# Linear attention and a SiLU MLP on one core: chunk 0 in two token parts, one more column group by Strassen's scheme, last sums per half

## The chip, the cores and the metric

The kernel runs on one core of one Trainium2 chip. The metric is the device time of an execution in microseconds (us). Eleven executions of the kernel before took 271.12 to 277.2 us, with a median of 275.72.

Engines are named as in the profile: PE (TensorE, matrix products), PEld (its weight loads), DVE (VectorE), ACT (ScalarE), POOL (GpSimd), SP (SyncE, which here only issues DMAs).

## The reference

Eight batches of 8 heads, 576 tokens, head size 64; then a two-layer MLP over all 4,608 tokens.

```python
q_s = softmax(q, over the head's 64 elements)
k_s = softmax(k, over the 576 tokens)
kv  = einsum('bhsd,bhse->bhde', k_s, v)          # 64 x 64 per head
x   = einsum('bhsd,bhde->bhse', q_s, kv)         # heads side by side: (4608, 512)
h   = x @ w_in                                   # (4608, 2048)
g   = h * (1.0 / (1.0 + exp(-h)))                # silu
out = g @ w_out                                  # (4608, 512), float32
```

## The kernel before

**Attention, per batch.** q, k and v of a batch are loaded as 128-partition tiles `qt`, `kt`, `vt` (one buffer each, so that a load waits for the last reader of the batch before). ACT takes the exponential (`exp`, L106) in two halves of four heads each (`cc` = 0, 1), DVE sums q's rows (`qsum`, L120 and L121), and `qnorm` (L126) multiplies; POOL does that for batches 1 to 7. `tr_dma` (L137) has a DMA transpose the normed q into `qT`; batch 0 is transposed on PE instead (`tr`, L149). `vcast` puts v as bf16 beside a column of ones, `kv` (L168) multiplies exp(k) with it, `kvcopy` (L180, L181) divides by the sums. `xt` (L203) multiplies qT by kv and `xtcopy` (L221, L223) writes the result to `XT`, x transposed, which is the MLP's input.

**The MLP, per chunk.** The tokens are cut into 9 chunks. XT of chunk 0 is made per batch, with 576 tokens, and worked in two pieces of 320 and 256 columns; chunk 1 brings 448 more, and the rest 512 each. (The second layer always takes 512 tokens.) The hidden 2,048 columns are 16 blocks `fb` of 128; four groups `g` of them, each two blocks of the lower and the two matching ones of the upper half, are the unit of Strassen's scheme.

- Chunks 0 and 1 run every block plainly: `mm1` (L233: four matmuls, 512 wide or the piece's width) and `act1`, in which ACT takes a tanh and DVE completes the silu (L247, L259).
- From chunk 2 on, some groups are plain (`std`: two in chunk 2, one in chunks 3 to 8; there ACT takes the silu at L263) and the others go by Strassen's scheme in Winograd's form: seven products of half size instead of eight. `product1` (L316) makes product k with four matmuls of 256 columns. Its left sides are blocks of `W1` or of the sums `TX` of such blocks (`vsum`, L291); its right sides are quarters of XT or their sums `XS` (`xsum`, L273 to L279: S1 = A10 + A11, S2 = S1 - A00, S3 = A00 - A10, S4 = A01 - S2). `sum1` (L333, L339, L341) adds the products up on DVE, one copy per group on DVE or ACT, and `silu1` (L355) writes `GT`.
- The second layer of chunk 0 is plain (`mm2`, L476). For chunks 1 to 8 it is Strassen's scheme too: `presum` (L369 to L375) makes the sums `SW` and rewrites a quarter of GT in place, `wsum` (L387) makes the sums `TW` of `W2` once, `product` (L411) multiplies in two halves `a` of 128 tokens, `after` (L428 and others) adds up on DVE, and `qstore` (L462, L465) has SP issue two DMAs per result, one for each half of the partitions.

The sums of a presum or xsum can run on DVE or POOL. MP and WP tiles are in the 8 PSUM banks: six in the ring that first-layer products, kv and xt share, two for the second layer.

**The order** is written out by hand in `PLAN`: for each chunk, steps with positions (`put`), sorted by position into a list, and issued to the engines in that order. Every engine works its instructions strictly in order. Positions of the second layer of chunk t (`y`, `ya`, `pb`) are in the list of chunk t + 1; the attention of batch b is in list b - 1. `order` is the sequence of (group, product); `xs`/`xe`, `pa`/`pae` and `pb`/`pbe` are positions and engines (0 DVE, 1 POOL) of xsum and of the presums of the first and the second half; `ex`, `qs`, `qn`, `tp`, `ox`, `oc` are positions of exp, qsum, qnorm, transpose, xt and xtcopy; `lq`, `lk`, `lv` of loads.

**The start.** SP issues q, k, v of batch 0 in halves (L97): q0, q1, k0, v0, k1, v1. POOL waits for v0 by a copy of one element (`gate`, L527) and then issues the weights (L516, L522) and batch 1, each casting weights to bf16:

```python
load_w1(0); load_w1(1); load_w2(0); load_w1(2); load_w2(1); load(1, "qt", q, eng=nc.gpsimd)
load_w1(3); load(1, "kt", k, eng=nc.gpsimd); load_w2(2); load(1, "vt", v, eng=nc.gpsimd); load_w2(3)
```

PE runs 24 warm-up matmuls (`heat`, L544), and eight more between the first steps.

Of the kernel before, what the change touches and what calls it, by code (L numbers as in the profile page):

```python
# [15 lines left out]
PLAN = {  # L16
    0: {'y': [5.5, 6.5, 7.5, 8.5, 8.5, 9.5, 10.5, 11.5, 13.5, 13.8, 14.5, 15.5, 15.6, 15.7, 15.9, 22.5], 'ex': [8.9, 10.9, 12.9, 13.4], 'qs': [9.92, 11.4], 'qn': [10.43, 11.41], 'vs': [14.45, 15.05], 'ks': [15.65, 15.75], 'kc': [15.651, 15.751], 'lq': 14.06, 'tp': 12.9, 'ox': [16.35, 16.6], 'oc': [16.36, 18.61], 've': [2, 2]},
    1: {'ex': [0.9, 4.4, 5.9, 5.4], 'qs': [3.9, 4.9], 'qn': [4.91, 5.91], 'vs': [9.3, 10.9], 'ks': [12.4, 13.9], 'kc': [13.41, 14.91], 'lq': 10.45, 'lk': 12.4, 'lv': 15.41, 'tp': 11.4, 'ox': [16.4, 23.6], 'oc': [17.91, 23.61], 've': [1, 1], 'pa': [13.1, 17.7, 18.3], 'pae': [1, 0, 0]},
    2: {'std': 2, 'order': [(3, 1), (2, 1), (2, 6), (3, 6), (2, 2), (2, 7), (3, 2), (3, 7), (3, 5), (2, 5), (2, 4), (3, 3), (3, 4), (2, 3)], 'y': [-2.5, 1.5, 3.5, 4.5, 5.5, 7.5, 9.5, 11.5, 14.0, 15.5, 17.5, 19.0, 20.0, 21.0], 'ex': [-2.6, 0.41, 2.92, 0.43], 'qs': [2.9, 3.9], 'qn': [5.91, 5.91], 'vs': [3.42, 12.4], 'ks': [8.9, 16.4], 'kc': [10.91, 16.41], 'lq': -0.55, 'lk': -2.1, 'lv': 14.41, 'tp': 7.4, 'ox': [18.4, 19.4], 'oc': [18.91, 19.41], 'sl': [0.5, 1.5, 3, 3, 4.5, 8.5, 7, 7], 'add': {(3, 2): 17.02, (2, 7): 13.55, (3, 1): 10.02, (3, 6): 11.55, (2, 5): 17.55, (2, 3): 21.55, (3, 3): 19.55}, 'act': {(2, 6): 13.02, (2, 4): 19.02, (2, 3): 25.02, (2, 5): 17.55, (3, 2): 14.55, (3, 3): 23.02, (2, 1): 11.55, (3, 1): 9.55, (2, 7): 16.02}, 's1': {2: 0, 3: 0}, 'xs': [0.4, 0.9, 7.9, 4.4], 'pa': [16.45, 23.95, 19.45], 'ya': {3: 22.45, 6: 5.5, 5: 15.95, 2: 7.95}, 'm1': [1, 0], 'pb': [-0.4, 0.2, 2.1, 2.2, 2.8], 'xe': [0, 1, 1, 1], 'pae': [1, 1, 1], 'pbe': [0, 0, 0, 0, 0], 've': [1, 2]},
}  # L20
STEADY = {'std': 1, 'order': [(1, 1), (1, 6), (1, 2), (1, 7), (1, 5), (2, 1), (2, 6), (1, 4), (1, 3), (2, 2), (2, 7), (2, 5), (3, 1), (2, 4), (3, 6), (2, 3), (3, 7), (3, 2), (3, 5), (3, 4), (3, 3)], 'y': [1.5, 3.5, 5.5, 7.5, 9.5, 10.0, 15.5, 16.5, 17.5, 18.0, 22.0, 23.5, 24.2, 24.6], 'ex': [-5.1, -0.59, -4.08, -4.57], 'qs': [5.4, 6.4], 'qn': [5.91, 6.41], 'vs': [0.4, 7.42], 'ks': [11.9, 17.4], 'kc': [15.91, 17.41], 'lq': 9.95, 'lk': 16.9, 'lv': 9.41, 'tp': 8.9, 'ox': [22.4, 22.4], 'oc': [22.91, 23.41], 'sl': [2.0, 2.0, 6.5, 4.0], 'add': {(2, 2): 17.02, (1, 2): 6.55, (3, 2): 20.55, (3, 1): 16.55, (3, 7): 21.02, (1, 5): 9.55, (3, 5): 22.55}, 'act': {(1, 5): 12.02, (2, 6): 12.02, (1, 2): 7.02, (3, 1): 19.02, (1, 6): 9.02, (1, 1): 8.02, (3, 3): 25.55, (3, 5): 25.02, (1, 3): 14.02, (2, 2): 15.02, (2, 5): 16.55, (1, 4): 13.02, (3, 7): 23.02, (3, 6): 20.02}, 's1': {1: 1, 2: 0, 3: 0}, 'xs': [-1.6, 0.9, -1.6, 1.4], 'pa': [21.45, 21.95, 23.45], 'pb': [-0.05, 2.46, 2.95, -0.04, 2.95], 'ya': {4: 23.95, 5: 19.45}, 'm1': [0, 0], 'xe': [0, 0, 0, 0], 'pae': [1, 0, 0], 'pbe': [0, 0, 0, 0, 1], 've': [1, 1]}
# [8 lines left out]
def kernel(  # L30
# [71 lines left out]
    def exp(b, src, dst, cc):  # L102
        if dst not in st[b]:
            st[b][dst] = ap.tile([128, J, NG * D], BF16, name=dst, bufs=1)
        o = st[b][dst][:, :, cc * 128:(cc + 1) * 128].rearrange("p j (g d) -> p j g d", d=D)
        nc.scalar.activation(out=o, in_=jgd(st[b][src], cc), func=ACT.Exp)  # L106

    def vcast(b, cc, eng):
        o = vaug.rearrange("p j (g e) -> p j g e", e=E1)[:, :, 2 * cc:2 * cc + 2, 0:D]
        if eng is nc.scalar:  # L110
            eng.copy(out=o, in_=jgd(st[b]["vt"], cc))
        else:
            eng.tensor_copy(o, jgd(st[b]["vt"], cc))

    def qsum(b, cc):
        if "zq" not in st[b]:
            st[b]["zq"] = ap.tile([128, 2, J, 2], FP32, name="zq")
            st[b]["rzq"] = ap.tile([128, 2, J, 2], FP32, name="rzq")
# [69 lines left out]
    def xt(t, cc, tags=("ring", "ring"), dve=0):  # L188
        if t not in XT:
            XT[t] = mp.tile([128, NC, S], BF16, name="XT")  # L190
        for i, (off, size) in enumerate(part[t]):
# [18 lines left out]
            if t == 0:  # L210
                xtcopy(t, cc, dve)
# [292 lines left out]
    for cc in range(2):  # L504
        load(0, "qt", q, cc)
# [182 lines left out]
```

The softmax here doesn't subtract the row's maximum and nothing guards it: scores larger than these inputs give would overflow.

## Time and profile before

| | |
|---|---|
| median of 11 runs | 275.72 us (271.12 to 277.2) |
| the profiled execution | 274.68 us; span of its instructions 272.9 us |
| granted TensorE clock, mean | 0.989 |
| first matmul of chunk 0 | 16.27 us |
| first xt of chunk 2 that uses batch 2 | 69.0 us |
| steady chunk (150.56 to 177.11) | 26.55 us |
| last matmul ends | 268.1 us |
| bytes moved by DMA | 46.48 MB, mean 170 GB/s |

Times count from the span's start. In a group's row stand line, engine, operation, output <- input with partitions x elements and type, the number of instructions, their busy time in us and mean duration in ns; then the idle time of the engine just before them and what ended it. A row of the chain of waits has start, length and what ran. A row of the stages has the stage, its length, then for each engine busy time and number of instructions, the granted clock, the DMA engines' share and GB/s. Instructions of one engine overlap a little: a sum of 686 ns starts some 0.61 us after the one before it.

### The profile page before, as it was taken

Reading aid. Unit: us, or ns where it says so; the run is one execution under the profiler, and the core shown is the slowest. Engines: PE = TensorE matmul, PEld = TensorE weight load, DVE = VectorE, ACT = ScalarE, POOL = GpSimd, SP = SyncE. Lnnn points to the kernel's source line nnn. Section 1 sums busy time; section 2 is a strip of 40 time slices with the busy share of each in tenths; the row PEclk is TensorE's granted clock in tenths of the full one; section 3 lists DMA queues with packets and bytes.
Section 4 is the critical chain, followed back from the end, with each engine's and each line's share of the span. In section 5 each row is a group of like instructions: output and inputs, shape, how many; then the busy total and the mean of one; then the engine's idle time right before and its main releaser. Section 6 shows DMA issues by size and latency. Waiting matters only on the chain.

```text
span 272.9 us, 6402 instructions
## 1 busy us (share of the span) xinstructions
PE 256.5 (94%) x2594; PEld 191.7 (70%) x2594; DVE 210.4 (77%) x405; ACT 172.7 (63%) x276; POOL 110.7 (41%) x71
## 2 busy tenths in 40 slices
PE   8689989975899999999999999999999999999992
PEld 3366645432568768886888688868886887788882
DVE  2976486498499898889888988889887668877932
ACT  5665576795896599648964996498654457344400
POOL 1552578996159745540644063416232013100000
PEclk9999999999799999999999999999999999999997
DMA  7999999989819750599059805971623012201324
GB/s 250 308 196 258 321 298 188 389 269 242 309 29 373 203 155 7 91 303 361 12 107 371 277 11 110 380 247 29 118 50 78 2 38 60 58 11 31 91 66 115
DMA packets 42925, 46.48 MB, mean 170 GB/s; under 512 B 18576, under 2 KB 30864, under 8 KB 42896
## 3 DMA queue, kind: packets, MB, share of 16 engines
q1 hardware_dynamic: 37856, 38.35, 47.6%
q0 software_dynamic: 5040, 7.73, 12.7%
q8 instruction: 20, 0.33, 0.5%
q14 instruction: 9, 0.07, 0.1%
HBM read 36.70 MB, written 9.44 MB: 169 GB/s over the span
## 4 chain that ended last, share of the span: by engine, by line
PE 64%; DMA 16%; POOL 6%; ACT 5%; issue 5%; SPq 2%; DVE 2%; POOLq 0%
PE ops L411 30%; PE hps L316 18%; PE hps L233 11%; DMA W<-in_moe_w_out_dram 8%; DMA kt<-in_k_dram 4%; POOL eq L126 3%; DMA qT<-eq 3%; PE ops L476 2%; PE kvps L168 1%; PE o L203 1%; ACT ek L106 1%; ACT eq L106 1%; POOL W L516 1%; ACT L263 1%; SPq L465 1%
## 5 line engine op out<-in xcount | busy, mean ns | idle before, releaser
L233 PE MATMUL hps<-XT,W 128*128 128x512 bf16 (+3 forms) x320 | 61.3, 337 | 1.9 <-DVE GT L259 1.7
L411 PEld LDWEIGHTS <-GT 128*128 128x128 bf16 x512 | 50.3, 98 | 9.3 <-issue 0.4
L233 PEld LDWEIGHTS <-W 128*128 128x128 bf16 x320 | 31.2, 98 | 25.6 <-issue 3.6
L411 PEld LDWEIGHTS <-SW 128*128 128x128 bf16 x384 | 37.2, 98 | 5.0 <-DVE SW L371 0.2
L355 ACT ACTIVATE GT<-u 128x512 bf16<-128x512 f32 x40 | 24.5, 629 | 23.8 <-DVE u L333 23.6
L126 POOL TENSOR_TENSOR eq<-eq,rzq 128x1152 bf16<-128x1152 bf16 x14 | 29.9, 2155 | 17.7 <-ACT GT L263 6.7
L316 PE MATMUL hps<-XS,TX 128*128 128x256 bf16 x240 | 35.0, 273 | 0.3 <-ACT GT L263 0.3
L316 PEld LDWEIGHTS <-TX 128*128 128x128 bf16 x320 | 30.6, 98 | 5.8 <-issue 2.1
L259 DVE SCALAR_TENSOR_TENSOR GT<-sg,hps 128x320 bf16<-128x320 f32 (+3 forms) x64 | 23.6, 414 | 13.2 <-ACT sg L247 12.6
L411 PE MATMUL ops<-W,GT 128*128 128x256 bf16 x256 | 33.7, 277 | 0.0
L411 PE MATMUL ops<-TW,SW 128*128 128x256 bf16 x256 | 33.0, 273 | 0.0
L411 PE MATMUL ops<-TW,GT 128*128 128x256 bf16 x256 | 32.9, 273 | 0.0
L333 DVE SCALAR_TENSOR_TENSOR u<-hps,s 128x512 f32<-128x512 f32 x40 | 27.2, 682 | 6.4 <-PE hps L316 4.9
L333 DVE SCALAR_TENSOR_TENSOR u<-hps,u 128x512 f32<-128x512 f32 x40 | 27.4, 686 | 4.0 <-PE hps L316 3.3
L375 POOL TENSOR_TENSOR SW<-GT,SW 128x1024 bf16<-128x1024 bf16 x6 | 13.9, 2320 | 40.2 <-DVE SW L371 28.7
L369 POOL TENSOR_TENSOR SW<-GT 128x1024 bf16<-128x1024 bf16 x7 | 14.9, 2131 | 35.7 <-PE ops L411 35.7
L247 ACT ACTIVATE sg<-hps 128x320 f32<-128x320 f32 (+2 forms) x48 | 21.2, 454 | 9.8 <-DVE GT L259 4.5
L316 PEld LDWEIGHTS <-W 128*128 128x128 bf16 x240 | 23.0, 98 | 3.3 <-issue 0.2
L120 DVE TENSOR_REDUCE zq<-eq 128x18 f32<-128x1152 bf16 x16 | 21.3, 1332 | 3.7 <-ACT eq L106 3.7
L316 PE MATMUL hps<-XT,W 128*128 128x256 bf16 x160 | 24.0, 273 | 0.0
L223 ACT CAST XT<-o 128x512 bf16<-128x512 f32 (+3 forms) x36 | 18.2, 561 | 7.6 <-PE o L203 7.6
L106 ACT ACTIVATE eq<-qt 128x1152 bf16<-128x1152 f32 x16 | 18.5, 1162 | 6.0 <-DMA qt<-in_q_dram 5.9
(77 smaller groups left out, 380.5 us busy)
## 6 DMA issues: line engine op xcount, KB each, us to landing
qt<-in_q_dram SPq DMA_DIRECT2D x6, 1152.0 KB, 8.3
kt<-in_k_dram SPq DMA_DIRECT2D x6, 1152.0 KB, 9.3
vt<-in_v_dram SPq DMA_DIRECT2D x6, 1152.0 KB, 6.5
W<-in_moe_w_in_dram POOLq DMA_DIRECT2D x4, 512.0 KB, 9.6
W<-in_moe_w_out_dram POOLq DMA_DIRECT2D x4, 512.0 KB, 17.8
out_dram<-u SPq DMA_DIRECT2D x16, 128.0 KB, 2.4
out_dram<-u SPq DMA_DIRECT2D x32, 64.0 KB, 2.1
qt<-in_q_dram SPq DMA_DIRECT2D x2, 576.0 KB, 4.0
```

The lines of the kernel that those rows point to most:

```text
L106: nc.scalar.activation(out=o, in_=jgd(st[b][src], cc), func=ACT.Exp)
L120: nc.vector.reduce_sum(out=st[b]["zq"][:, cc], in_=e, axis=AX.X)
L126: eng.tensor_tensor(out=e, in0=e, in1=r[:, :, :, None].to_broadcast([128, J, 2, D]), op=ALU.mult)
L223: nc.scalar.copy(out=x, in_=o1[g][:, 0:size])
L233: nc.tensor.matmul(out=hps[:, 0:size], lhsT=W1[:, c, fb * 128:(fb + 1) * 128], rhs=XT[t][:, c, off:off + size], start=(c == 0), stop=(c == ...
L247: nc.scalar.activation(out=sg[:, 0:size], in_=hps[:, 0:size], func=ACT.Tanh, scale=0.5)
L259: nc.vector.scalar_tensor_tensor(out=y, in0=sg[:, h], scalar=1.0, in1=hps[:, h], op0=ALU.add, op1=ALU.mult)
L316: nc.tensor.matmul(out=o[:, f, :], lhsT=l(c, 2 * g + f), rhs=r(c), start=bool(first and f == 0 and c == 0), stop=(c == HK - 1), skip_group ...
L333: nc.vector.scalar_tensor_tensor(out=out, in0=o, scalar=1.0, in1=x, op0=ALU.mult, op1=ALU.add)
L355: nc.scalar.activation(out=y, in_=MP[t, g, x], func=ACT.Silu)
L369: V.tensor_add(S1[:, f], quad(t, 0, f, 1), quad(t, 1, f, 1))
L411: nc.tensor.matmul(out=o[:, a, :], lhsT=l(f), rhs=r(f), start=bool(first and a == 0 and f == 0), stop=(f == HF - 1), skip_group_check=True,)
```

## The change

Three edits, and a new `PLAN` with all positions and engine choices.

1. **Chunk 0 in two token parts.** q of batch 0 is loaded in two parts: token groups 0 to 4 of the nine first (320 of 576 tokens), the others behind k and v. exp, qsum, qnorm, tr, xt and mm1 of chunk 0 take a part as argument. PE starts mm1 on the first part; the rest of q goes through exp, norm, transpose and xt between those blocks (`rest`, `resttr`, `restx`). The 32 half blocks come in an order of their own. The weights' order is a list, the first 512 columns of W1 in two DMAs, W2's last quarter ahead of batch 1's v; the gate waits for the second half of k. The eight later warm-up matmuls are gone.
2. **All four groups by Strassen's scheme** in chunks 3 to 8 (`std` 0 instead of 1). In the new PLAN three of four xsums and six of eight presums of these chunks are on POOL (before: none and two). `kvcopy` and `xtcopy` take an engine from the plan.
3. **Last sums per half.** The last result of chunk 8 is added and stored per half of 128 tokens (`last`), with its two DMAs on SP and on ACT.

```diff
-STEADY = {'std': 1, 'order': [(1, 1), (1, 6), (1, 2), (1, 7), (1, 5), (2, 1), (2, 6), (1, 4),
...
-'xs': [-1.6, 0.9, -1.6, 1.4], 'pa': [21.45, 21.95, 23.45], 'pb': [-0.05, 2.46, 2.95, -0.04, 2.95],
...
-'xe': [0, 0, 0, 0], 'pae': [1, 0, 0], 'pbe': [0, 0, 0, 0, 1]
+STEADY = {'std': 0, 'order': [(0, 1), (0, 6), (0, 5), (0, 7), (1, 1), (0, 2), (0, 4), (1, 6),
...
+'xs': [-2.4, -1.3, -13.6, 1.9], 'pa': [20.95, 30.95, 33.45], 'pb': [1.45, 1.46, 5.95, 1.46, 1.95],
...
+'xe': [1, 1, 1, 0], 'pae': [1, 1, 1], 'pbe': [0, 0, 1, 1, 1]
...
+WORDER = ['w11', 'w10', 'w12', 'w21', 'w20', 'w13', 'q', 'w14', 'k', 'w22', 'w23', 'v']
+GATE = ('kt', 1)
...
-    def load(b, name, src, ccs=None, eng=nc.sync):
+    def load(b, name, src, ccs=None, eng=nc.sync, js=(0, J)):
...
-        eng.dma_start(out=st[b][name][:, c, :], in_=x[:, c, :])
+        e = slice(js[0] * D, js[1] * D)
+        eng.dma_start(out=st[b][name][:, c, e], in_=x[:, c, e])
...
+    def last(a):
+        t = NCH - 1
+        o, q = WP[t, "C"], WP[t, "u2"]
+        nc.vector.scalar_tensor_tensor(
+            out=q[:, a, :], in0=o[:, a, :], scalar=1.0, in1=q[:, a, :], op0=ALU.mult, op1=ALU.add
+        )
+        for half, eng in enumerate((nc.sync, nc.scalar)):
+            b, j = divmod(8 * t + 4 * a + half, J)
+            row = out[b * S:(b + 1) * S, HM:2 * HM].rearrange("(p j) o -> p j o", j=J)
+            eng.dma_start(out=row[:, j, :], in_=q[half * P:(half + 1) * P, a, :])
...
     for cc in range(2):
-        load(0, "qt", q, cc)
+        load(0, "qt", q, cc, js=J0)
     for cc in range(2):
         load(0, "kt", k, cc)
         load(0, "vt", v, cc)
+    load(0, "qt", q, js=J1)
...
+            f = slice(*((0, 256), (256, 512), (512, 1024), (1024, 1536), (1536, 2048))[int(name[2])])
...
     for cc in range(2):
-        exp(0, "qt", "eq", cc)
-        qsum(0, cc)
-        qnorm(0, cc, nc.vector)
+        exp(0, "qt", "eq", cc, J0)
+        qsum(0, cc, J0)
+        qnorm(0, cc, nc.vector, J0)
+        tr(0, cc, J0)
...
+    def rest(cc):
+        exp(0, "qt", "eq", cc, J1)
+        qsum(0, cc, J1)
+        qnorm(0, cc, nc.vector, J1)
+
+    def resttr(cc):
+        tr(0, cc, J1)
+        trc(0, cc, J1)
+
+    def restx(cc):
+        xt(0, cc, 1)
+        xtcopy(0, cc, 1)
...
+            order = p["order"] if t == 0 else [(fb, 0) for fb in range(NFB)]
+            for x, (fb, i) in enumerate(order):
+                put(t, x, mm1, t, fb, i)
+                put(t, x, act1, t, fb, i)
...
+            if t == NCH - 1 and m == 3:
+                put(t + 1, x, last, a)
```

The order of chunk 0's half blocks, as (fb, part), begins (2, 0), (0, 0), (5, 0), (3, 0), (6, 0), (4, 0), (1, 0), (7, 0), (1, 1), (3, 1), (2, 1), (0, 1), (4, 1), (6, 1), (5, 1), (7, 1), (8, 1), (8, 0), (9, 1), (12, 0). w10 and w11 are columns 0 to 255 and 256 to 511 of W1, w12 to w14 its further quarters, w20 to w23 the quarters of W2's rows.

## The prediction

> **What bounds the kernel now.** I read the busy shares first, then the slices, then stages, the chain of waits by time, the groups by shape, and single timelines. The page's first lines and slices:
>
> ```profile
> PE 256.5 (94%) x2594; PEld 191.7 (70%) x2594; DVE 210.4 (77%) x405; ACT 172.7 (63%) x276; POOL 110.7 (41%) x71
> ...
> PE   8689989975899999999999999999999999999992
> ...
> DMA  7999999989819750599059805971623012201324
> ```
>
> TensorE (PE) is full from slice 12 (75 us) to the last; its holes lie in the first 70 us, where the DMA row is full too. Stages (us, then busy time of PE, PEld, DVE, ACT, POOL) of the end of chunk 1 and of two steady chunks:
>
> ```profile
> 50.10:69.00 18.90, 13.47 (x137) 6.66 (x137) 14.49 (x30) 12.52 (x20) 15.23 (x9) 0.99 0.98 292
> 150.56:177.11 26.55, 26.55 (x303) 21.53 (x301) 23.34 (x45) 20.30 (x32) 11.08 (x6) 1.00 0.60 189
> 177.11:203.66 26.55, 26.55 (x303) 21.52 (x301) 22.91 (x45) 19.86 (x32) 9.85 (x5) 1.00 0.44 116
> ```
>
> A steady chunk lasts 26.55 us, all of it PE; DVE has 3.4 us to spare, POOL 16. So a matmul less is time, as long as no other engine gets late. In 50 to 69 us PE lacks 5.4 us, and the chain says why:
>
> ```profile
> 59.53 2.12 POOL eq L126
> 61.67 7.29 DMA qT<-eq
> 69.00 0.96 PE o L203 x12
> ...
> 74.62 1.73 PE hps L233 x8
> ...
> 85.56 0.87 PE hps L316 x8
> ```
>
> Chunk 2 waits for batch 2's q: landed, exponentiated, normed on POOL, transposed by DMA, used by PE at 69.0. The last two rows give PE's pace: 0.216 us for a 512-wide matmul, 0.109 for a 256-wide one.
>
> **Part 1: group 0 by Strassen in chunks 3 to 8.** Counted in the built programs: the 512-wide matmuls of L233 go from 128 to 32, so 16 less per chunk (3.46 us); 28 products of 256 columns come in (3.05 us). PE: -0.41 us per chunk, -2.46 in six. What the seven products need besides, from these rows:
>
> ```profile
> L333 DVE SCALAR_TENSOR_TENSOR u<-hps,u 128x512 f32<-128x512 f32 x40 | 27.4, 686 | 4.0 <-PE hps L316 3.3
> L369 POOL TENSOR_TENSOR SW<-GT 128x1024 bf16<-128x1024 bf16 x7 | 14.9, 2131 | 35.7 <-PE ops L411 35.7
> L371 DVE TENSOR_TENSOR SW<-SW,GT 128x1024 bf16<-128x1024 bf16 x15 | 11.0, 733 | 0.1
> L275 POOL TENSOR_TENSOR XS<-XS,XT 128x512 bf16<-128x512 bf16 x1 | 1.2, 1153 | 6.2 <-DVE XS L273 6.2
> ```
>
> DVE gains five sums and one copy per chunk (6 x 0.62 back to back = 3.7 us). To pay for them, the plan sends four of DVE's six presums (4 x 0.62) and three of four XS sums (3 x 0.38) to POOL, together 3.6: DVE stays near 23 of now 26.1 us. ACT trades four silu of 605 ns for four of 630: nothing. POOL per steady chunk: six presums at 2.13 (two of them perhaps 2.42), three XS sums at 1.15, two norms at 2.1, one cast at 1.17, together 22 to 23 us instead of 10 to 11. It still fits on average; the question is order. Before, a chunk opened with two plain blocks (1.73 us) needing only XT; now its second product (0,6) needs S2 of the new XS, three POOL sums behind XT, and POOL is in order: SW, SW, GT, S3, S1, S2.
>
> I follow that chain by PE's order in the list of a chunk, time 0 at its first product. The last product whose silu frees POOL's first presum, (1,3), ends its sum behind (2,7) at 15.3 + 0.1 + 0.68 + 0.62 = 16.7; silu 0.63: 17.4. POOL: 2.13 + 2.13 + 2.12 = 23.8, then S3, S1, S2 at 1.15 = 27.25, with 0.2 for the handovers 27.4. PE wants S2 at 26.1 + 1.3 = 27.4. No slack. Now a second cost: DVE sums with two SBUF sources wait for a running POOL operation.
>
> ```profile
> 74.89 1.16 POOL L113 CAST vaug<-vt 128x1152 bf16<-128x1152 f32 x1 [1.58 <-DMA vt<-in_v_dram]
> 75.27 1.33 DVE L373 TENSOR_TENSOR GT<-GT 128x1024 bf16<-128x1024 bf16 x1
> ```
>
> The sum issued at 75.27 takes 1.33 instead of 0.68: it starts when POOL's cast ends at 76.05. In the new chunk three such DVE sums stand behind (0,6), while POOL runs its 2.13 us SW sum right after S2: DVE arrives 1.25 us after S2 and waits 0.9. From there DVE has (back to back) 1.7 + 14 x 0.61 + 2 x 1.56 us of work up to the sum of (1,3): it ends 15.5 us after S2, so the loop S2 to S2 is 15.5 + 0.75 + 10.05 = 26.3 instead of PE's 26.1. I take 0.25 us given back at each of four boundaries: +1.0. Bounds: 0 (handovers shorter, DVE not late) and +2.1 us per boundary (a whole POOL operation in the way each time). A second loop, POOL's norms to the transpose to the next xt, comes out likewise: norm ends at 14.6, landing 5.6 (median; 7.3 the longest), so 20.2 to 21.9 against xt at 21.8; covered, at 0.1 in the worst. Chunks 7 and 8 have no exponentials, norms or casts: their 0.41 each stays whole.
>
> The Trainium skill (GPSIMD Engine Reference, its opening and Key points) says that VectorE is about twice as fast at elementwise work, so that such work belongs there; that speaks against the six presums on POOL. The rows above say 3.1 times (2131 against 687 undisturbed). With a factor of two POOL's chain would be some 3 us shorter, the 1.0 given back would be nought and the sum -4.6.
>
> **Part 2: the start.** The two halves of q0 shrink to five ninths. A 576 KB piece lands every 1.5 us (k at 8.2, v at 9.7, k at 11.2, v at 12.6), so k and v come 1.3 us earlier and the first matmul of chunk 0 at 15.0 instead of 16.27. POOL's gate now waits for the second k (11.2 - 1.3 = 9.9 instead of 9.7), and q0's rest joins the queue: W does not come earlier. From the DMA issues' times to landing, the blocks land at 15.6, 18.2, 21.4, 24.0, 26.5 (W), 30.7 (q1), 33.1, 36.1 (k1), 38.4, 41.4, 43.8. In the new order the third matmul block needs the columns that land at 18.3 (before: W in order, no wait), the first mm2 the slot at 24.0, and fb 12 the slot at 33.2. PE work of the list is 31.6 us in both, plus 1.1 us of transposes and xt for the second part, now behind PE's start. Followed block by block PE waits 2 us at the third, then reaches fb 12 at 32.4 and waits 0.8, and ends the list at 50.6 to 51.5, against 49.1 now. That 1.5 to 2.4 us loss falls into the hole before 69.0: chunk 1 has 12 us of PE work and 18.9 us to do it. What sets 69.0 is batch 2's q. Its chain gets shorter: batch 1's second exp 34.2 instead of 33.5, but its sum follows at once on DVE, norm 37.1 to 39.3 (before 38.2 to 40.5), transpose issue 39.3, q2's load 43.6 instead of 44.45, its landing 51.4; the second exp 54.7 (55.5), sum to 57.6 (59.4). POOL by then has 8 sums since 41.0 (w23 is one slot earlier), to 56.2, and the norms end at 60.5 instead of 61.67. I take -1.2 for the start. Bounds: -3 (transpose lands in 5.6 instead of 7.3 and q2 earlier still) and +2 (the late list not absorbed). The W pieces of 256 columns have 1 KB rows, and no load here shows such; nearest are k's of 2.3 KB at 1.5 us per 576 KB, and I count no loss.
>
> **Part 3: the end.**
>
> ```profile
> 268.14 0.69 DVE L428 SCALAR_TENSOR_TENSOR u<-ops,u 128x512 f32<-128x512 f32 x1 [1.05 <-PE ops L411]
> 268.86 1.24 SPq L462 DMA_DIRECT2D out_dram<-u  x2
> ```
>
> After the last matmul (268.12) a 512-wide sum, then two issues one behind the other on SP, then 2.1 to 2.5 us of landing. Now 256 wide (between 0.35 for 192 and 0.48 for 320: 0.41), and the second issue (0.62) stands on ACT, idle there: -0.28 - 0.62 = -0.9. Bounds -0.3 and -1.2. The Trainium skill (DMA: Bandwidth & Descriptors, Rules for kernel authors) says that two transfers to disjoint partition halves serialize and aren't worth splitting; by it the transfer gains nothing, and if the issue gained nothing either the term would be -0.3.
>
> **Other edits**: kvcopy and XT copies by plan on ACT or DVE (0.28 and 0.55 us) are in the counts; the 8 warm-up matmuls taken away lay in PE time that waits for k and v; the granted clock is 1.00 there, and should it fall to the 0.94 of the stage from 69 to 96 us for 10 us, that is 0.6 us.
>
> **Sum.** -2.46 + 1.0 - 1.2 - 0.9 = -3.6 us. The profiled execution took 274.68 (span 272.9, 1.8 around it), which would give 271.1. The median of the 11 runs is 275.72, 0.4% more; from it 272.1, and I say 272.
>
> **Rivals.** (A) Slower: POOL becomes the bound at each chunk's start. S2 is late by a whole POOL sum, 2.1 us at five boundaries, +10.5 against 4.6 of gains: 281. For it: no slack in the chain, POOL's load doubled, DVE's sums waiting as at 75.27. Against it: POOL has 3 us per chunk to spare and S1 to S2 run when DVE has no such sum. It decides from 0.9 us of lateness per boundary (4.6 / 5); at 1.5 it is 1% slower. Chance 0.16. (B) The start's loss isn't absorbed: list 0 ends 2.4 us later and chunk 2 starts 1.7 later instead of 1.2 earlier: -0.7 in all, 275. For it, the waits for W above; against, the 5.4 us hole. Chance 0.18. (C) Nothing given back and a start at its bound: -2.46 - 3 - 0.9 = -6.4, 269.3. Chance 0.16. That the change doesn't do what it says is excluded by the counts: 96 wide matmuls gone, 168 narrow ones there.
>
> **How the numbers follow.** My forecast 0.5. About 1% (2.7 us, below 273.0 or above 278.5) is what a measurement of this kernel can tell from no change. Of the forecast's 0.5 two thirds lie below 273.0, with C: faster 0.50. The other third and most of B: within 0.32. A and a little of B: slower 0.18. The range 267.5 to 278 leaves out the far end of A and little beyond C's.
>
> **What would show it.** PE's period in chunks 4 to 6: 26.1 to 26.4 is right, over 27 with POOL before PE's (0,6) is A. XT of chunk 2 by PE at 67 to 68.5 is the start right; 70 or later is B. POOL's three XS sums at 1.15 and its busy time near 180 us; DVE's presums at the chunk's start above 0.7. The last PE matmul to the span's end about 3.8 instead of 4.8 us. If mm1's wait for W is absent, my slots were wrong.

## The result and the profile after

| | before | changed |
|---|---|---|
| median | 275.47 us (47 executions, 271.09 to 277.61) | 279.24 us (12 executions, 277.44 to 281.09) |
| ratio | | 1.0214, 95% interval 1.0171 to 1.0256 |
| profiled execution; its span | 274.68; 272.9 us | 280.04; 278.3 us |

The change makes the kernel 2.1% slower; 1.3% faster had been forecast. Medians here and below are over all executions; a ratio leaves out those more than 1.5% above the fastest of the same kernel, which takes away 17 of the 28 of the kernel before beside e11_all and none of e11_all's 12, so that a median and a ratio can tell different things. The two profiled executions differ by 5.4 us, the medians by 3.8.

Three marks cut the two spans into four stretches: the start of the 12 matmuls of xt(2) that need batch 2's q (called xt(2) below), the second xt of chunk 3, and PE's last matmul.

| stretch | before | changed | difference |
|---|---|---|---|
| start to xt(2) | 69.0 | 74.0 | +5.0 |
| to chunk 3's second xt | 26.5 | 24.7 | -1.8 |
| to PE's end ("the steady stretch") | 172.6 | 175.5 | +2.9 |
| to the span's end | 4.8 | 4.1 | -0.7 |

The page of the changed kernel, first lines and slices (6.96 us each):

```profile
PE 258.3 (93%) x2658; PEld 199.9 (72%) x2658; DVE 220.8 (79%) x403; ACT 178.8 (64%) x287; POOL 177.6 (64%) x109
...
PE   8468999999899999989998999999999999999993
...
PEclk9755999999999999999999999999999999999999
DMA  6899996898927961499249905981522012110334
```

POOL's load is as predicted (near 180 us). New are the PEclk digits 7, 5, 5 in the second to fourth slice, and the 8s in the PE row at 118 and 146 us, where there were none after 75 us. The stages (stage, its length, busy time of PE, PEld, DVE, ACT, POOL, the granted clock, the DMA engines' share, GB/s), one in the start and two steady chunks:

```profile
12.00:26.00 14.00, 9.28 (x81) 4.62 (x71) 8.63 (x22) 5.32 (x11) 8.57 (x12) 0.50 1.08 162
...
125.04:152.39 27.35, 26.58 (x313) 22.70 (x313) 23.51 (x42) 21.38 (x31) 21.29 (x13) 1.00 0.69 209
152.39:179.55 27.16, 26.58 (x312) 22.67 (x312) 23.50 (x42) 21.37 (x31) 21.18 (x13) 1.00 0.67 181
```

A steady chunk takes 27.2 to 27.4 us instead of 26.55, of which PE works 26.58. What it waits for stands in the chain of waits:

```profile
58.72 1.12 PE hps L236 x5
...
61.12 1.27 DVE zq L127
62.69 1.00 DVE GT L262 x2
63.69 1.27 DVE zq L127
...
65.40 2.11 POOL eq L135
67.51 0.03 POOL vaug L119
67.54 6.41 DMA qT<-eq
73.95 0.04 issue
74.00 0.57 PE o L208 x12
...
138.97 4.16 POOL eq L135 x2
143.13 0.02 issue
143.15 9.20 DMA qT<-eq
152.34 0.04 issue
152.39 0.49 PE o L208 x12
```

The upper rows are the chain into xt(2). Its end is the same steps as in the kernel before, norms ending at 67.5 instead of 61.67; ahead of them stand DVE's sums of batch 2's q (`zq`), which wait in DVE's order behind the silu of chunk 1's first blocks (`GT`), and those behind PE. The lower rows are new: in a steady chunk the DMA transpose takes 9.20 us to land, and PE's xt waits for it. The landings of chunks 4, 5, 6 are 9.3, 9.2, 9.0 us; before they were 5.5, 4.6, 6.5.

Last the two timelines that belong to the start, of PE and of POOL:

```profile
11.42 0.71 PE L169 MATMUL kvps<-vaug,ek 64*64 64x65 bf16 x36 [2.56 <-ACT vaug L117]
...
16.89 1.33 PE L236 MATMUL hps<-XT,W 128*128 128x320 bf16 x4
19.42 1.25 PE L236 MATMUL hps<-XT,W 128*128 128x320 bf16 x4 [1.20 <-DMA W<-in_moe_w_in_dram]
21.93 2.32 PE L236 MATMUL hps<-XT,W 128*128 128x320 bf16 x8 [1.26 <-DMA W<-in_moe_w_in_dram]
...
11.75 0.18 POOL L545 COPY gate<-kt 1x1 f32<-1x1 f32 x1 [10.44 <-DMA kt<-in_k_dram]
...
21.96 0.76 POOL L100 DMA_DIRECT2D qt<-in_q_dram  x1 [5.43 <-ACT eq L110]
```

PE is idle for 2.56 us before the first kv, the clock falls to a half inside this hole (at 10.8 us), and four matmuls of 320 columns take 1.33 us. PE waits twice for W. POOL stands 5.43 us at the issue of batch 1's q load: that load needs q's buffer, and the buffer's last reader, the exponential of q0's rest, stands on ACT behind an activation that waits for mm1, which waits for W. The kernel before had this in the same place:

```profile
16.27 6.05 PE L233 MATMUL hps<-XT,W 128*128 128x320 bf16 x48
22.16 1.03 PE L476 MATMUL ops<-W,GT 128*128 128x512 bf16 x4
```

There 48 matmuls of chunk 0 are through by 22.16; in the changed kernel the 48th is through at 31.4.

### The profile page after: what moved, and what is told of

The parts are those of the page before. It is cut to its first block, busy times and chain, and to the rows that moved or that the text cites. A ratio compares the mean times of both kernels' runs of the same rounds, so it can differ in the third digit from the quotient of the medians.

```text
span 278.3 us, 6614 instructions
## 1 busy us (share of the span) xinstructions
PE 258.3 (93%) x2658; PEld 199.9 (72%) x2658; DVE 220.8 (79%) x403; ACT 178.8 (64%) x287; POOL 177.6 (64%) x109
## 3 DMA queue, kind: packets, MB, share of 16 engines
HBM read 36.70 MB, written 9.44 MB: 166 GB/s over the span
## 4 chain that ended last, share of the span: by engine, by line
PE 64%; DMA 15%; DVE 8%; POOL 6%; issue 4%; ACT 1%; POOLq 0%; DVEq 0%; ACTq 0%
PE ops L414 27%; PE hps L319 20%; DMA qT<-eq 12%; PE hps L236 9%; PE ops L490 5%; POOL eq L135 4%; DMA W<-in_moe_w_in_dram 3%; DVE u L336 2%; DVE zq L127 2%; PE o L208 2%; DVE SW L372 1%; PE kvps L169 1%; POOL GT L376 1%; POOL vaug L119 1%; DVE SW L374 1%
## 5 line engine op out<-in xcount | busy, mean ns | idle before, releaser
L336 DVE SCALAR_TENSOR_TENSOR u<-hps,s 128x512 f32<-128x512 f32 x52 | 35.4, 682 | 15.9 <-PE hps L319 15.8
L358 ACT ACTIVATE GT<-u 128x512 bf16<-128x512 f32 x52 | 32.6, 628 | 22.6 <-DVE u L336 21.9
L236 PE MATMUL hps<-XT,W 128*128 128x320 bf16 (+3 forms) x224 | 43.0, 339 | 3.8 <-DMA W<-in_moe_w_in_dram 2.5
L319 PE MATMUL hps<-XS,TX 128*128 128x256 bf16 x312 | 45.1, 273 | 0.8 <-DVE XS L278 0.8
L319 PEld LDWEIGHTS <-TX 128*128 128x128 bf16 x416 | 39.8, 98 | 7.7 <-issue 1.7
L262 DVE SCALAR_TENSOR_TENSOR GT<-sg,hps 128x192 bf16<-128x192 f32 (+3 forms) x64 | 24.3, 414 | 11.5 <-ACT sg L250 10.5
L378 POOL TENSOR_TENSOR SW<-GT,SW 128x1024 bf16<-128x1024 bf16 x11 | 23.5, 2139 | 8.5 <-DVE SW L374 7.0
L376 POOL TENSOR_TENSOR GT<-GT 128x1024 bf16<-128x1024 bf16 x12 | 25.5, 2126 | 0.0
L127 DVE TENSOR_REDUCE zq<-eq 128x18 f32<-128x1152 bf16 (+2 forms) x18 | 21.8, 1212 | 3.4 <-ACT eq L110 3.4
L358 ACT ACTIVATE GT<-s 128x512 bf16<-128x512 f32 x26 | 16.3, 627 | 9.7 <-DVE s L336 9.7
```

Of the source, the lines that this page charges most:

```text
L127: nc.vector.reduce_sum(out=st[b]["zq"][:, cc, js], in_=e, axis=AX.X)
L236: nc.tensor.matmul(out=hps[:, 0:size], lhsT=W1[:, c, fb * 128:(fb + 1) * 128], rhs=XT[t][:, c, off:off + size], start=(c == 0), stop=(c == ...
L262: nc.vector.scalar_tensor_tensor(out=y, in0=sg[:, h], scalar=1.0, in1=hps[:, h], op0=ALU.add, op1=ALU.mult)
L319: nc.tensor.matmul(out=o[:, f, :], lhsT=l(c, 2 * g + f), rhs=r(c), start=bool(first and f == 0 and c == 0), stop=(c == HK - 1), skip_group ...
L336: nc.vector.scalar_tensor_tensor(out=out, in0=o, scalar=1.0, in1=x, op0=ALU.mult, op1=ALU.add)
L358: nc.scalar.activation(out=y, in_=MP[t, g, x], func=ACT.Silu)
```

## The experiments

All spans are of single profiled executions, in us; "stretch" is the steady stretch, "end" from PE's end to the span's end. Where xt(2) had no wait between its first four and the other 12 matmuls, the mark is the start of all 16.

| run | xt(2) | chunk 3's xt | stretch | end | span | clock | median | ratio to before (95%) |
|---|---|---|---|---|---|---|---|---|
| before | 69.0 | 95.5 | 172.6 | 4.8 | 272.9 | 0.989 | | |
| changed | 74.0 | 98.7 | 175.5 | 4.1 | 278.3 | 0.967 | 279.24 | 1.0214 (1.0171 to 1.0256) |
| e1_start | 72.5 | 97.3 | 172.8 | 4.7 | 274.8 | 0.974 | 276.36 | 1.0141 (1.0027 to 1.0255) |
| e2_strassen | 68.4 | 93.6 | 176.1 | 4.8 | 274.5 | 0.994 | 277.22 | 1.0129 (0.9998 to 1.026) |
| e3_tail | 68.5 | 96.0 | 173.4 | 4.2 | 273.6 | 0.985 | 275.69 | 1.0119 (1.0028 to 1.0209) |
| e4_swap | 71.4 | 96.1 | 173.6 | 4.1 | 273.8 | 0.980 | 277.54 | 1.0152 (1.004 to 1.0263) |
| e15_early | 72.5 | 97.2 | 173.6 | 4.5 | 275.4 | 0.974 | 277.26 | 1.0173 (1.0127 to 1.0218) |
| e14_ahead | 67.8 | 94.5 | 172.0 | 4.8 | 271.3 | 0.990 | 275.44 | 1.0087 (1.0035 to 1.0139) |
| e5_heat | 71.7 | 96.9 | 174.4 | 4.0 | 275.4 | 0.987 | 277.24 | 1.0094 (1.0033 to 1.0154) |
| e6_rest | 72.4 | 97.2 | 175.7 | 4.0 | 276.9 | 0.971 | 278.91 | 1.0206 (1.0148 to 1.0265) |
| e7_gate | 71.8 | 96.5 | 175.1 | 4.1 | 275.7 | 0.974 | 277.07 | 1.0131 (1.0058 to 1.0204) |
| e13_only | 71.2 | 95.9 | 174.8 | 4.1 | 274.8 | 0.974 | 277.05 | 1.0121 (1.004 to 1.0202) |
| e8_mended | 70.6 | 95.9 | 173.6 | 4.1 | 273.6 | 0.989 | 274.93 | 1.0085 (1.0041 to 1.0129) |
| e10_order | 69.5 | 94.6 | 173.6 | 4.1 | 272.3 | 0.995 | 273.52 | 0.9998 (0.9949 to 1.0048) |
| e9_split | 69.4 | 96.2 | 172.6 | 4.9 | 273.7 | 0.989 | 275.88 | not given |
| e11_all | 67.2 | 93.0 | 172.7 | 4.7 | 270.4 | 0.999 | 273.28 | 0.9999 (0.9949 to 1.0049) |
| e12_mix | 68.4 | 95.1 | 174.0 | 4.7 | 273.8 | 0.994 | 274.78 | 1.004 (0.9984 to 1.0096) |

Single executions scatter by several us (271.09 to 277.61 in the kernel before), and each kernel has one profile: the same start gave xt(2) at 74.0, 72.5, 71.4 and 72.5 (changed, e1, e4, e15). The stretch repeats better: 172.6 to 172.8 with the old plan (before, e1, e9; e3_tail and e14_ahead lie outside) and 173.6 in four runs with the new plan and early transposes. So the stretch decides below where it can, the start only by more than its scatter. The median of the kernel before, run beside each group, was 272.71 (e1 to e4), 273.99 (e5 to e8), 275.34 (e9 to e12), 273.96 (e13, e14) and 275.70 us (e15); medians of different groups are not to be compared as they stand.

### Each part alone

The changed start with the old plan of chunks 3 to 8; the new plan with the old start; the new end with all else old:

```diff
 e1_start: changed kernel with
-STEADY, PLAN[8] of the changed kernel;  put(t + 1, x, last, a)
+STEADY, PLAN[8] of the kernel before
 e2_strassen: kernel before with
+STEADY, PLAN[8] of the changed kernel
 e3_tail: kernel before with
+    put(t + 1, x, last, a)
```

> The new start alone: lists 0 to 2 of the change with the old plan of chunks 3 to 8 (group 0 plain, presums on DVE) and the old end. Theory (the start costs 5 us): PE's first xt on batch 2's q at about 74 us as in the changed kernel, period of steady chunks 26.5 as before, 280 to 281 us against 275.5. Rival (the start's loss is an effect of the whole plan and mostly absorbed): 276 to 277.

xt(2) at 72.5, stretch 172.8 as before. The late start belongs to the start alone; it costs 1.4% (0.3 to 2.6). The time, 276.36, is the rival's, but 3.7 us above the kernel before beside it.

> The old kernel with only the new plan of chunks 3 to 8: group 0 by Strassen's scheme, presums and xsums on POOL, q's load directly ahead of the transpose. Theory (the transpose lands late behind q's load): transposes of chunks 3 to 5 take about 9 us to land, the period is 27.2 to 27.4, chunks 7 and 8 are shorter by 0.4, and the time is 0.5 to 1.5 us over that of before. Rival (the body costs nothing, the start alone is at fault): 2.5 us below before.

xt(2) as before, stretch 176.1 instead of 172.6, transposes landing in 7.7, 9.0 and 10.1 us. The new plan alone costs 3.5 us in the stretch where a gain had been forecast, of which PE's waits for the transpose are 2.2 us. (The interval of its ratio still takes in 1.00, and the rival's 2.5 us of gain is not there.)

> The old kernel with only the last sums per half and the two store queues. From the last PE matmul to the end of the span 4.1 us instead of 4.8: -0.7 us. Rival (two transfers of partition halves gain nothing): -0.3 or less. Either is inside what the timing can tell; the profile's last rows decide.

From PE's end 4.2 instead of 4.8 us, but the stretch is longer. From the last xt (chunk 8) to the span's end it is 273.6 - 227.3 = 46.3 us, against 272.9 - 226.7 = 46.2: nothing gained. The timeline of this run's end shows what gives it back:

```profile
267.88 0.43 DVE L456 SCALAR_TENSOR_TENSOR u<-ops,u 128x256 f32<-128x256 f32 x1 [0.18 <-PE ops L411]
268.34 2.04 ACTq L462 DMA_DIRECT2D out_dram<-u  x2
268.36 1.03 PE L411 MATMUL ops<-W,SW 128*128 128x256 bf16 x8 [0.52 <-DVE u L456]
269.07 1.43 SPq L462 DMA_DIRECT2D out_dram<-u  x2
269.43 0.42 DVE L456 SCALAR_TENSOR_TENSOR u<-ops,u 128x256 f32<-128x256 f32 x1 [1.12 <-PE ops L411]
```

PE waits 0.52 us for DVE's first half sum before it makes the second half: both halves are one PSUM tile. What this execution's span has more than that of the kernel before comes elsewhere: from xt(2) to chunk 3 it took 27.5 instead of 26.5 us, at a lower clock. Whether the ratio of 1.0119 has to do with the edit stays open.

### The transpose and the load

In the changed plan SP issues the next q load 0.75 us ahead of the transpose. e4_swap puts it behind; e15_early puts it ahead of the four stores that stand before it; e14_ahead puts it ahead of the transpose in the kernel before, where it stood behind.

```diff
 e4_swap, STEADY of the changed kernel
-'lq': 9.95
+'lq': 15.45
 e15_early, STEADY of the changed kernel
-'lq': 9.95
+'lq': 2.95
 e14_ahead, STEADY of the kernel before
-'lq': 9.95
+'lq': 8.85
```

> The changed kernel with one position changed: in chunks 3 to 7 SP issues the load of the next batch's q behind the transpose instead of ahead of it. Theory (late transpose): its landing falls from 9.0 to 9.3 us to 4.6 to 6.6, the period from 27.3 to 26.2 to 26.6, the time by 2.5 to 3.5 us to 276 to 277. Rival (POOL's chain of six presums and three XS sums sets the period, with DVE's sums waiting for POOL): the landing falls but the period stays over 27, the time within 0.7 us of the changed kernel's.

Landings 5.1, 4.6, 6.1 us, no wait of PE for them, periods 26.6 to 26.7, stretch 173.6: the mechanism is right and worth 1.9 us in the stretch, less than the 2.5 to 3.5 us expected of the time (the ratio falls from 1.0214 to 1.0152). Against the kernel before the stretch is still 1.0 too long.

> The kernel before with one edit: in chunks 3 to 7 the next q load is issued on SP directly ahead of the transpose instead of behind it. In the kernel before the transposes of chunks 4 to 6 landed in 5.5, 4.6 and 6.5 us. Theory 'load ahead': they now land in 8 to 10 us as in the changed kernel, with the plan of chunks as before, so the order on the queue makes the difference and not the larger load of POOL or DVE. Rival: the landing stays under 7 us, and what lengthened it in the changed kernel is something else in its plan. Time: since the transposes are issued earlier in this plan than in the changed one, 0 to 2 us longer.

The edit missed its aim: in this plan the load was issued 7 us ahead of the transpose and had landed by then (5.4 us), and the transposes landed in 5.6, 4.6 and 6.4 us. Neither theory had that case; it asks whether the place on the queue matters at all, or only a load in flight. (Its stretch is 0.6 us shorter than that of the kernel before: there PE waits at 134 us for a silu, here it does not. Its profiled execution, 273.08 us, is one of its faster ones; what makes its ratio 1.0087 is not in that profile.)

> The changed kernel with one edit: in chunks 3 to 7 the next q load is issued on SP ahead of the four c stores instead of behind them, so some 5 to 8 us ahead of the transpose instead of 0.75. Theory 'load in flight': by then the load has landed or nearly, the transposes of chunks 4 to 6 land in 4.6 to 7 us instead of 9.0 to 9.3, PE waits for them 0.3 us or less in all, and the chunks' period is 26.6 to 26.8 instead of 27.2 to 27.4. Rival 'any load ahead on the queue': landings of 8 us or more stay, and the period with them.

Its SP timeline, and that of the changed kernel in the same chunk:

```profile
131.96 0.39 SPq L100 DMA_DIRECT2D qt<-in_q_dram  x1
137.43 2.39 SPq L479 DMA_DIRECT2D out_dram<-c  x4
140.95 2.76 SPq L145 DMA_TRANSPOSE qT<-eq  x1
```

```profile
139.90 2.38 SPq L479 DMA_DIRECT2D out_dram<-c  x4
142.33 0.59 SPq L100 DMA_DIRECT2D qt<-in_q_dram  x1
143.15 5.57 SPq L145 DMA_TRANSPOSE qT<-eq  x1
```

With the load 9 us ahead, landings are 5.8, 4.7 and 6.2 us and the stretch is 173.6, as in e4_swap. The rival falls: what the transpose waits behind is the load in flight, not a place on the queue. In the changed kernel the issuing instruction itself is held too, 5.57 instead of 2.76 us on SP's queue.

### The start

Four mends of the changed kernel, singly and together:

```diff
 e5_heat
+    heat(12)
     exp(0, "kt", "ek", 0)
...
+    heat(5)
     kv(0, 1)
     kvcopy(0, 1)
+    heat(2)
     xt(0, 1, 0)
 e6_rest, PLAN[0]
-'r': [-0.5, 1.5]
+'r': [-0.5, -0.4]
 e7_gate
-GATE = ('kt', 1)
+GATE = ('vt', 0)
 e13_only, PLAN[0] 'order'
-(2, 0), (0, 0), (5, 0), (3, 0), (6, 0), (4, 0), (1, 0), (7, 0)
+(2, 0), (3, 0), (0, 0), (1, 0), (5, 0), (6, 0), (4, 0), (7, 0)
```

e8_mended is the changed kernel with the edits of e4_swap, e5_heat, e6_rest and e7_gate; e10_order has that of e13_only as well.

> The changed kernel with 19 warm-up matmuls more in its start: 12 behind the transposes of q's first part, 5 ahead of the second kv, 2 ahead of the second xt. Marker: the time at which PE begins the 12 matmuls of xt(2) that wait for the DMA transpose of batch 2's q: 69.0 in the kernel before, 74.0 in the changed one (72.5 and 71.4 in two other runs with the same start). Theory 'clock' (PE's gaps in the start lower the clock, and slow mm1 holds everything behind it): granted clock 1.00 from 8 to 28 us, eight 512-wide mm1 matmuls at about 22 us take 1.9 us or less instead of 2.3 for 8 halves, POOL's wait at q1's load ends by 19, marker at 69.5 to 71, time 2 to 3 us below the changed kernel's 279. Rival 'loads': clock 1.00, but PE waits for W just as late; the wait of POOL ends at 20 to 22 as before and the marker stays in 71.4 to 74.

The clock is 1.00 to 16 us, then falls all the same (0.88, 0.50, 0.77 in the next three stretches of 4 us): PE waits 2.3 us for W at that point. POOL's wait ends at 19.67, xt(2) is at 71.7: as the rival has it, within the scatter of unmended starts.

> The changed kernel with one number moved: the second half of q0's rest is exponentiated and normed ahead of the list of chunk 0 instead of behind its second block, so the last reader of the q buffer no longer stands behind an activation that waits for W. Theory 'POOL queue': POOL's wait at the issue of batch 1's q load, 5.43 us (to 21.96) in the changed kernel, falls to about 1 us (q0's rest lands at 14.6, two exps to about 17), q1's load is issued at 17 to 18 and lands at 29 to 31 instead of 33.1, the transpose of batch 1 is issued at 41.5 to 43.5 instead of 45.8, marker (xt(2)) 2 to 3 us earlier, at 69.5 to 71.5. Rival: q1's load then shares bandwidth with the W pieces that PE waits for, these land 1 to 2 us later, the marker moves by less than 1 us.

POOL waits 2.05 instead of 5.43 us and issues q1's load at 17.89, but PE waits 3.2 us for W and xt(2) is at 72.4. The rival holds: the wait on POOL's queue was real and not what set xt(2) alone.

> The changed kernel with POOL's gate for the W loads on the first half of v0 instead of the second half of k0. Theory 'gate': gate at 9.5 to 10.7 instead of 11.75 (10.5 in the best run with this start), W pieces land 1 to 1.5 us earlier, marker (xt(2)) 1 us earlier than in the runs with the same start (71.4 to 74.0). Rival: bandwidth is the limit, so k0's second half, v0's second half and q0's rest land later by what W gains; kv(0,1) and the rest exp move later and the marker is not earlier.

Gate at 9.85, xt(2) at 71.8: not told apart from the scatter.

> The changed kernel with all four mends: warm-up matmuls, q0's rest early, gate on v0's first half, and the q load behind the transpose on SP in chunks 3 to 7. If the three causes of the late start add up, marker (xt(2)) at 68 to 70 and time 272.5 to 275, no slower than the kernel before; if a fourth cause is left (bandwidth), marker over 71 and time over 276.

xt(2) at 70.6, between the two cases (70 and 71), with one listed wait for W of 2.6 us left and a clock of 0.88 from 12 to 26 us. The time, 274.93, is in the first case's range; the wait for W is what the four mends left.

> All four mends of e8_mended, and in chunk 0 the blocks 3 and 1, which read columns of W that have landed, stand ahead of block 5, at which PE waited 2.6 us for W. Marker (first matmul of xt(2)) was 70.6 in e8_mended, 69.0 in the kernel before; the long run of chunk 1's matmuls began at 55.2, 49.1 before. Theory 'one token part eats W faster than it lands': the wait falls to under 1 us, chunk 1's run begins at 53 to 54, marker 69 to 69.6. Rival: PE waits as long for the next pieces (W lands at the same pace whatever the order), chunk 1's run begins at 54.5 or later, marker over 70.2.

No listed wait for W, clock 1.00 throughout, chunk 1's run of matmuls from 54.0, xt(2) at 69.5, as the theory has it. Its stage and its PE rows against those of the changed kernel above:

```profile
12.00:26.00 14.00, 10.89 (x141) 5.83 (x140) 10.53 (x28) 6.28 (x16) 8.79 (x11) 1.00 1.25 200
...
17.83 2.06 PE L236 MATMUL hps<-XT,W 128*128 128x320 bf16 x14 [0.20 <-DVE XT L224]
20.02 0.40 PE L153 MATMUL qtps<-ident,eq 128*128 128x128 bf16 x4
20.26 0.71 PE L236 MATMUL hps<-XT,W 128*128 128x320 bf16 x4
```

The blocks that read landed columns run through without a hole, and the blocks behind them find their W there. The ratio to the kernel before is 0.9998 (0.9949 to 1.0048); over all executions the medians are 273.52 and 275.34.

> The changed kernel with one edit: in chunk 0 the blocks 3 and 1 stand ahead of block 5, whose columns of W land late. In four runs with the changed start PE waited 2.2 to 3.3 us for W, chunk 1's run of matmuls began at 55.5 to 58.0 and xt(2) at 71.4 to 74.0. Theory 'order': the wait for W is the main cause of the late start, so it falls to 1 us or less and xt(2) comes at 70 to 71.5, also with the low clock. Theory 'clock': the low clock, with POOL's wait at q1's load, is the main cause and order matters only with warm-up matmuls; PE reaches the waiting block later because the blocks ahead of it run at half clock, and xt(2) stays at 71.5 to 74.

The order alone: PE's wait 1.25 us at 19.28, clock 0.54 from 12 to 26 us, chunk 1's run from 55.1, xt(2) at 71.2. Between the two theories: the edge of what 'order' expected, and just outside the scatter of the unmended starts. The order and the clock do not add up as separate terms: without warm-up matmuls the clock is low whatever the order, and with them (e5_heat) the wait for W brings it down. What each is worth by itself stays open; that all four edits to the start together (warm-up matmuls, q0's rest, gate, order) bring xt(2) from 71.4 to 74.0 down to 69.5 (67.2 in e11_all, with the same start) is shown.

### The end, and all together

e9_split gives the last two halves of e3_tail a PSUM tile each. e11_all is e10_order with that and with (1, 1) ahead of (0, 6) in chunk 8, where PE waited 0.8 us for an XS sum. e12_mix is the same with the old start and no mends to it.

```diff
+        two = t == NCH - 1 and bank == "C"
+        key = (t, bank, a) if two else (t, bank)
-        if first and a == 0:
+        if first and (two or a == 0):
...
 e11_all, e12_mix, PLAN[8] 'order'
-(0, 1), (0, 6), (0, 2), (0, 7), (1, 1)
+(0, 1), (1, 1), (0, 6), (0, 2), (0, 7)
```

> The kernel before with the new end, and the last sums' PSUM tile split into one tile per half. In the end alone (e3_tail) PE waited 0.52 us for the first half's sum before the second half's matmuls, and from the last xt to the span's end it took 46.3 us against 46.2 in the kernel before. Theory 'shared tile': the wait stands there because both halves are one PSUM tile; with two tiles it is gone and that stretch takes 45.5 to 45.7. Rival: the two halves wait for DVE for another reason (the sum of u3 ahead, a bank that is not free), the wait of 0.4 us or more stays and the stretch is 46 or more.

The timeline of its end:

```profile
267.80 1.25 SPq L484 DMA_DIRECT2D out_dram<-s  x2
267.96 0.42 DVE L467 SCALAR_TENSOR_TENSOR u<-ops,u 128x256 f32<-128x256 f32 x1 [0.18 <-PE ops L414]
268.42 1.35 ACTq L473 DMA_DIRECT2D out_dram<-u  x2
268.83 0.42 DVE L467 SCALAR_TENSOR_TENSOR u<-ops,u 128x256 f32<-128x256 f32 x1 [0.45 <-PE ops L414]
269.15 1.53 SPq L473 DMA_DIRECT2D out_dram<-u  x2
```

Half right. PE's wait is gone and the last sum starts at 268.83, 0.6 us earlier than in e3_tail. But from the last xt to the span's end it is still 273.7 - 227.4 = 46.3, so PE's wait was not what held the end. What fits is SP: its two s stores occupy it from 267.80 to 269.05, and then its two u stores to 270.68, 43.3 us behind the last xt. In the kernel before SP's last issue ended 43.4 us behind the last xt (270.10), in e3_tail 43.2. Halving the result doubled its stores, so SP has as many as before. No run moves a store off SP to test it.

> e10_order with the split end of e9_split, and in chunk 8 the product (1,1) ahead of (0,6), at which PE waited 0.8 to 0.9 us for an XS sum. Expected: neither wait in the trace, from chunk 3's second xt to PE's end 172.2 to 172.6 us (e4_swap 173.6, before 172.6), span 271 to 272.5, time 1 to 2 us below e8_mended's. Rival: (0,6) is then late behind another POOL or DVE sum, and the stretch stays at 173 or more.

Stretch 172.7, the wait for the XS sum halved (0.4 us), the tail's wait gone, time 1.65 us below e8_mended's. By the ratio it is level with the kernel before (0.9999, 0.9949 to 1.0049), not better. Over all executions its median is 273.28 against 275.34, with clocks of 0.995 to 1.00 against 0.978 to 1.00; whether the new start is what spares it the lower clocks was not tested.

> The start of the kernel before, with the changed chunks 3 to 8, the q load behind the transpose, the order of chunk 8 as in e11_all, and the split end. If the parts add: marker (xt(2)) 68.5 to 69.0, from chunk 3's second xt to PE's end 172.2 to 172.6, PE's end to the span's end 4.1, so a span 1 us below that of the kernel before on the same chip, and a ratio of 0.990 to 1.000. If Strassen's scheme in all four groups costs time by itself even with its waits mended, the stretch is 173 or more and the ratio over 1.002.

Stretch 174.0, beyond the 173 that was to mean that Strassen's scheme in all four groups costs time by itself. But its waits were not mended here: with the old start another XS sum is late (0.8 us behind POOL), and five presums make PE wait 0.2 us each. So the parts don't add, and whether the scheme costs time by itself is not decided. By the ratios no version here is shown to beat the kernel before.

## Why the prediction was wrong

**The start, forecast -1.2, measured +5.0 to xt(2) and +3.2 to chunk 3.** Four steps failed.
- "the granted clock is 1.00 there, and should it fall to the 0.94 [...] for 10 us, that is 0.6 us". It was 0.50 from 12 to 26 us. The text took the eight warm-up matmuls to lie in time that only waits; the 2.56 us hole they leave, and the holes behind it, cost the clock. And 0.94 was no bound: it is a mean over 27 us, in which the trace has 6 us at 0.74 (the stage shown below).
- "the third matmul block needs the columns that land at 18.3". The gate fired at 11.75 (10.5 to 11.9 in the runs with this start), not 9.9: the second half of batch 0's k was still in flight together with v's second half and q0's rest, which the prediction had join the queue without slowing what stands ahead of it. And w12 took 8.3 us to land: 21.9, so it was 3.6 us late, 2.0 of them by the gate. The two 256-column pieces ahead of it, for which no loss had been counted, landed at 16.1 and 19.4; PE waited for the second of them too.
- The list's end at 50.6 to 51.5: chunk 1's run of matmuls began at 57.95, against 49.07 before. A loss of 8.9 us doesn't fit into a hole of 5.4. And the hole was not free: the forecast had batch 2's q independent of PE's list, but in the chain above its sums on DVE stand behind the silu of chunk 1's blocks, and these behind PE. Rival B, the loss that isn't absorbed, is what happened, at three times its price.
- Moving q0's rest behind mm1 moved a queue: batch 1's q load on POOL now waits for the rest's exponential, and all that POOL issues behind it. It was issued at 21.96 instead of 13.71, and batch 1's transpose at 45.77, where 39.3 had been forecast. The text followed the list on PE, DVE and ACT, and gave POOL's issues the old times. By e6_rest this alone does not set xt(2).

**A gain not forecast, -1.8** between xt(2) and chunk 3. In the kernel before, the clock falls at 68.7 us, at the end of the 2.48 us hole before 69.0 that the text counted as free room; its stage behind xt(2), columns as above:

```profile
69.00:75.00 6.00, 6.00 (x39) 3.56 (x39) 2.28 (x5) 5.42 (x8) 1.26 (x2) 0.74 0.80 303
```

6 us at 0.74 are 1.6 us lost. In the changed kernel no hole on PE between 58 and 74 us is longer than 0.78 us, and the clock stays at 1.00.

**Chunks 3 to 8, forecast -1.46, measured +2.9.** "A second loop, POOL's norms to the transpose to the next xt [...] covered" is the step that failed most: it took landings of 5.6 to 7.3 us from the old order on SP, and the changed plan puts a 1,152 KB load 0.75 us ahead of the transpose. With 9.2 us the loop ends at 23.8 in the prediction's own count, against xt at 21.8 (PE's wait was 0.8 us at most, so the count itself was on the late side). Shown by e4_swap and e15_early: 1.9 us of the stretch. Another 0.5 is the wait that the end adds, below.

The other loop, S2 to S2, was seen rightly and taken too short: 26.3 us forecast, 26.64 measured. The prediction had DVE arrive 1.25 us behind S2 and be held by POOL's running sum. In the timelines of e11_all (POOL, DVE, PE) S2 ends at 123.55:

```profile
122.39 1.16 POOL L278 TENSOR_TENSOR XS<-XS,XT 128x512 bf16<-128x512 bf16 x1
123.51 2.13 POOL L378 TENSOR_TENSOR SW<-GT,SW 128x1024 bf16<-128x1024 bf16 x1
...
124.85 1.34 DVE L372 TENSOR_TENSOR SW<-GT 128x1024 bf16<-128x1024 bf16 x1
126.29 0.69 DVE L374 TENSOR_TENSOR SW<-SW,GT 128x1024 bf16<-128x1024 bf16 x1
...
123.60 0.60 PE L319 MATMUL hps<-XS,TX 128*128 128x256 bf16 x4
...
127.04 0.61 PE L417 MATMUL ops<-TW,SW 128*128 128x256 bf16 x4 [0.22 <-DVE SW L374]
```

DVE's sum is issued 1.30 us behind S2, takes 1.34 instead of 0.68, and PE waits 0.22 for the next. From the four matmuls before (126.22) to these it is 0.82 us for work of 0.44, so 0.38 is given back, where 0.25 had been put in. And the loop does set the pace, though the list of waits doesn't name it: S2 ends at 123.55, 150.19, 176.84 and 203.48, and each time PE's (0,6) begins 0.05 to 0.06 us behind it and as much later than the matmul before allows. The forecast took DVE's way round the loop (26.3) and PE's (26.1, no slack) side by side; the hold on DVE makes PE wait, so its cost is added to PE's way, which had nothing to spare. The term of 0.41 per chunk follows from counts that hold (three chunks of the steady stretch have 672 matmuls of 256 columns and none of 512, in the kernel before 588 and 48), and all of it went: 26.64 us against 26.55 before.

"Chunks 7 and 8 [...] their 0.41 each stays whole" failed too, by the 0.8 us wait for an XS sum in chunk 8. e11_all's stretch should be 2.4 us shorter than that of the kernel before (0.41 in each of six chunks) and is as long. Counted from the start of a matmul to the start of the next, four waits like the one above give 1.5 of it, what is left of the XS wait 0.6, waits for S2 0.2 and short waits for sums of DVE 0.7; on the other side the kernel before has a wait of 0.6 at 134 us that e11_all has not. That adds up to about the 2.4. Rival A, a whole POOL sum of 2.1 us at each chunk start, is not what happened: S2 was 0.05 to 0.06 us late there, and POOL stood idle 3.7 us per chunk ahead of its first presum, waiting for the silu of (1,3).

**The end, forecast -0.9, measured 0.** The part that was costed is there (4.1 to 4.2 us from PE's end, 3.8 forecast). The term that failed is the second issue: "the second issue (0.62) stands on ACT" was no gain, since SP still has two stores of that result and ends 43.2 to 43.4 us behind the last xt with the old end and both new ones. What was missed besides is a wait that the edit adds: DVE reads the first half while PE wants to write the second into the same tile, and PE waits. It moves PE's end by 0.5 us, but taking it away (e9_split) gained nothing at the span's end. The Trainium skill (PSUM — Partial Sum Buffer, PSUM bank collisions raise a hardware error) has a rule that points to such a wait: accesses of two engines are to be guarded by bank, not by address. The runs fit it: 0.52 us with one tile (e3_tail), no wait with two (e9_split); what unguarded halves would do, no run here shows.

## What to carry over

A part of the work that starts earlier on half the tokens uses up the weights nearly twice as fast (320 of 576 tokens per block here): count what PE can do with each piece that has landed, and order the blocks by it. Of a load that is moved, look at what is issued within the next few microseconds on the same DMA engines, and at whose buffer it waits for on its own queue; a hole on PE that looks like free room may also be costing its clock, and another engine's queue may carry the lateness past it. When a result is cut in two, check that the halves share no PSUM tile, and count the stores on each queue again.

## What was new about the hardware

- **The clock.** In the changed kernel it fell to 0.50 at 10.8 us, inside a hole on PE of 2.56 us (8.86 to 11.42), and came back at 27.9; from 12 to 26 us PE was busy for 9.28 of 14 us, with no listed hole over 1.26 us. The Trainium skill (TensorE: Matmul & The Clock Gate, HAM oscillation — how this bites in real kernels) asks for no idle gap over about 3.4 us. The level of one half agrees; as a limit it is not enough here, since no hole of the changed kernel reached it. The clock records of all 17 traces say more. Every change lies on a grid of 3.41 us (counted from the first rise), and the clock stayed low for 3.41, 6.83, 10.24, 13.65 or 17.07 us. Of the grid's steps at full clock, those ahead of a fall before the end of PE's work had PE busy for 5 to 48%, and no fall came after one with 53% or more, but for one of 67% in e5_heat. What ends a low stretch is less clear: 85 to 100% busy ahead of a rise, but 92 and 94% left it low in e13_only and e7_gate.
- **A DMA transpose behind a load in flight.** With 1,152 KB issued 0.75 us ahead it landed in 9.0 to 9.3 us in the changed kernel; with 3 to 5 us (batches 2 and 3, before and after) in 6.4 to 7.3; with 0.7 to 1.1 us in e2_strassen and e5_heat in 7.7 to 10.1; with 7 to 9 us in 4.6 to 6.4; with the load behind it in 4.6 to 6.5.
- **Loads that cast are counted by the bytes written.** While mostly weights run, the view has 202 GB/s at a share of 1.21 (the kernel before, 12 to 26 us), and 397 GB/s at 1.05 where plain loads run (8.86 to 11.42 us of the changed kernel). Each W load is listed with 512 KB, its size in bf16; the page's 36.70 MB read from HBM are q, k, v and both weights in float32. So by bytes read the casting loads are, as an estimate, about as fast as the plain ones (2 x 202).
